# Twenty short TensorE trains, read by nothing, behind the last store of an attention-and-FFN kernel

## The chip, the core and the metric

The kernel runs on one core of one Trainium2 chip. The metric is device time in microseconds (us) of one execution, and the figure before is the median of two runs. A profile was taken of one further execution; its time and its span (from the first to the last instruction) are given below. Engines: PE is TensorE's matmul, PEld its weight load, DVE is VectorE, ACT is ScalarE, POOL is GpSimd, SP is SyncE, which issues most of the DMA transfers.

## The reference

A per-head dynamic convolution over 7 neighbouring rows (8 x 4096 rows of 192 numbers, 8 heads, weights by a softmax over the 7 taps), and then a feed-forward layer with a squared ReLU. Everything is in 32-bit floats.

```python
w = exp(weight_gen - max); w = w / (sum(w) + 1e-09)          # 8 x 4096 x 8 heads x 7 taps
out = np.einsum('bshk,bskhg->bshg', w, x_unf)                # 7 shifted rows of x
x = out.reshape(32768, 192)
h = x @ w_in                                                 # 192 x 2048
g = np.maximum(h, 0.0) ** 2
return (g @ w_out).astype(np.float32)                        # 2048 x 192
```

## The kernel before, in words

The 32768 rows are cut into 64 chunks `c` of 512 rows. DVE makes the seven products of the convolution and adds them; a DVE transpose and a trip through DRAM turn the result so that the 192 features lie on partitions. For each chunk there are two matrix products:

- `mm1(c, j)` (line 446), for 8 values of `j`: `x @ w_in`, into two PSUM banks of the pool `ps_h` (four banks, tile `ph`).
- `mm2_turned(c, fb)` (line 519), for 16 values of `fb`: `g @ w_out`, into the four banks `acc0` to `acc3` of the pool `ps_o`.

Every number is kept as a high part and a low part in the type `fp32r`, so that a product is three matmuls (high by high, low by high, high by low). `W` holds `w_in` and `V` holds `w_out` in that form; `gh`, `gl` and `xh`, `xl` are the activations. Each matmul uses only 64 of TensorE's 128 rows: the work is issued in pairs, one matmul on partitions 0 to 63 and one on 64 to 127, into two different banks. Both halves are told by `h` (or `i`) in

```python
for h in range(2):
    rows = slice(h * D1, (h + 1) * D1)
    nc.tensor.matmul(accs[c][b + h], w, two_streams(g[rows]), **fl)
```

The moving operand, 512 columns, isn't read in the order of its addresses, but in two streams that take turns, 16 numbers (64 bytes) apart:

```python
def two_streams(t):
    return t.rearrange("p (b i m) -> p b m i", i=2, m=Q // 2)
```

So the columns come from the addresses 0, 16, 1, 17, 2, 18 and so on up to 15, 31, and then on in the next 32 numbers. The last chunk's second product is not turned: `mm2` (`mm2_tile`, line 492) holds the activations fixed on all 128 rows and moves `V` in the order of its addresses, 384 columns against the high part and 192 against the low part. In chunk 0 `mm2_tile` (line 483) does it in plain `fp32`, 192 columns at a time.

The program is written in the order in which each engine takes it (a manual schedule; no scheduler changes it). At its end stand, on PE, four matmuls at line 784 and eight at line 787 (192 columns each, all 128 rows); then a DVE addition (line 790), and `store(c, t, TC)`, the last of the output's DMA transfers (line 78). After that all engines meet and the program ends. `D1` is 64, `P` 128, `N` 512, `NF` 16, `D` 192, `Q` 32; `ghs[NCH - 1, NF - 1]` is the last high part of the last chunk, `accs[NCH - 1][0]` its bank `acc0`.

Of the kernel before, what the change touches and what calls it, by code (L numbers as in the profile page):

```python
# [8 lines left out]
F32 = mybir.dt.float32  # L9
# [12 lines left out]
def kernel(  # L22
# [547 lines left out]
    def store(c, t0, t1):  # L570
        put_out(c, t0, t1, outs[c][0], 1 if c == 0 else 0)
# [218 lines left out]
    nc.vector.tensor_tensor(out=o_sb[:, t], in0=rest[:, 0:D], in1=tmp[:, t, 0:D], op=ALU.add)  # L790
    store(c, t, TC)


# [1 line left out]
_INS = ["x", "weight_gen", "moe_w_in", "moe_w_out"]  # L795
# [26 lines left out]
```

## Time and profile before

| | us |
|---|---|
| median of 2 runs | 2129.09 (2128.73 to 2129.44) |
| profiled execution, its time | 2128.85 |
| profiled execution, its span | 2126.9 |
| PE busy in the span | 2121.8 |
| DVE busy | 1864.2 |
| ACT busy | 1797.9 |
| mean granted TensorE clock | 1.000 |

Time lies outside the span too: 2128.85 less 2126.9. A matmul's end is modelled in the profile, and matmuls overlap in the pipeline, so the busy time of PE doesn't tell its rate; the distance from one start to the next does.

### The profile page before, as it was taken

Reading aid. Unit: us, or ns where it says so; the run is one execution under the profiler, and the core shown is the slowest. Engines: PE = TensorE matmul, PEld = TensorE weight load, DVE = VectorE, ACT = ScalarE, POOL = GpSimd, SP = SyncE. Lnnn points to the kernel's source line nnn. Section 1 sums busy time; section 2 is a strip of 40 time slices with the busy share of each in tenths; the row PEclk is TensorE's granted clock in tenths of the full one; section 3 lists DMA queues with packets and bytes.
Section 4 is the critical chain, followed back from the end, with each engine's and each line's share of the span. In section 5 each row is a group of like instructions: output and inputs, shape, how many; then the busy total and the mean of one; then the engine's idle time right before and its main releaser. Section 6 shows DMA issues by size and latency. Waiting matters only on the chain.

```text
span 2126.9 us, 50423 instructions
## 1 busy us (share of the span) xinstructions
PE 2121.8 (100%) x19486; PEld 1865.2 (88%) x19486; DVE 1864.2 (88%) x2869; ACT 1797.9 (85%) x3492; POOL 9.9 (0%) x18
## 2 busy tenths in 40 slices
PE   9999999999999999999999999999999999999999
PEld 9888888888888888888888888888888888888888
DVE  9988888888888888888888888888888888888884
ACT  8888888888888888888888888888888888888886
POOL 0000000000000000000000000000000000000000
PEclk9999999999999999999999999999999999999999
DMA  8433334333343343433434433344334343333422
GB/s 231 99 72 85 92 97 102 86 69 100 91 100 92 65 104 86 99 94 67 100 87 98 105 78 77 91 100 100 86 70 104 87 99 91 68 101 86 100 66 49
DMA packets 324160, 195.33 MB, mean 92 GB/s; under 512 B 224984, under 2 KB 282328, under 8 KB 320080
## 3 DMA queue, kind: packets, MB, share of 16 engines
q1 hardware_dynamic: 322624, 188.58, 35.9%
q0 software_dynamic: 1296, 3.54, 0.9%
q8 instruction: 152, 2.49, 0.5%
q14 instruction: 88, 0.72, 0.1%
HBM read 106.39 MB, written 49.55 MB: 73 GB/s over the span
## 4 chain that ended last, share of the span: by engine, by line
PE 99%; ACT 0%; POOL 0%; issue 0%; DVE 0%; POOLq 0%
PE acc L519 50%; PE ph L446 46%; PE acc L483 1%; PE acc L492 1%; PE acc L446 0%; PE acc L355 0%; PE acc L581 0%; ACT rg L467 0%; ACT gh L471 0%; PE ph L343 0%; ACT rg L461 0%; PE ph L787 0%; PE acc L343 0%; PE acc L784 0%; DVE o_sb L790 0%
## 5 line engine op out<-in xcount | busy, mean ns | idle before, releaser
L519 PE MATMUL acc<-gh,V 64*128 64x512 f32 x5952 | 976.9, 376 | 0.0
L446 PE MATMUL ph<-xh,W 64*128 64x512 f32 x6084 | 822.4, 376 | 0.3 <-ACT rg L461 0.3
L463 ACT ACTIVATE rg<-ph 128x512 f32<-128x512 f32 x992 | 539.3, 596 | 303.8 <-PE ph L446 303.8
L519 PE MATMUL acc<-gl,V 64*128 64x512 f32 x3968 | 752.7, 376 | 0.0
L475 DVE TENSOR_TENSOR gl<-rg,gh 128x512 fp32r<-128x512 f32 x1008 | 641.2, 675 | 12.8 <-ACT gh L471 12.8
L446 PEld LDWEIGHTS ph<-xh,W 64*128 64x128 f32 x6084 | 576.1, 186 | 82.3 <-issue 0.7
L519 PEld LDWEIGHTS acc<-gh,V 64*128 64x128 f32 x5952 | 563.5, 186 | 78.8
L467 ACT ACTIVATE rg<-rg 128x512 f32<-128x512 f32 x1008 | 580.3, 632 | 0.2
L471 ACT CAST gh<-rg 128x512 fp32r<-128x512 f32 x1008 | 575.8, 627 | 3.3 <-PE acc L492 3.3
L519 PEld LDWEIGHTS acc<-gl,V 64*128 64x128 f32 x3968 | 375.6, 186 | 53.1 <-DVE gl L475 0.6
L280 DVE TENSOR_TENSOR pr<-xt,wt 128x768 f32<-128x768 f32 (+1 forms) x441 | 416.6, 946 | 2.2
L446 PE MATMUL ph<-xl,W 64*128 64x512 f32 x3042 | 411.4, 376 | 0.0
L293 DVE TENSOR_TENSOR pr<-pr 128x768 f32<-128x768 f32 x366 | 348.1, 951 | 2.2
L446 PEld LDWEIGHTS ph<-xl,W 64*128 64x128 f32 x3042 | 288.3, 186 | 40.1
L324 DVE TENSOR_TENSOR xl<-xT,xh 128x512 fp32r<-128x512 f32 x186 | 117.5, 687 | 114.2 <-ACT xh L321 114.1
L529 DVE TENSOR_TENSOR raw<-acc,raw 128x512 f32<-128x512 f32 x124 | 79.9, 687 | 94.7 <-ACT raw L527 94.7
L321 ACT CAST xh<-xT 128x512 fp32r<-128x512 f32 x186 | 102.5, 623 | 0.8 <-DMA xT<-xd 0.8
L527 ACT COPY raw<-acc 128x512 f32<-128x512 f32 x124 | 66.5, 597 | 0.0
L409 DVE STREAM_TRANSPOSE xr<-pr 128x768 f32<-128x768 f32 x61 | 59.7, 978 | 2.1
L541 DVE STREAM_TRANSPOSE raw<-raw 64x512 f32<-64x512 f32 x62 | 43.6, 703 | 2.1
L538 DVE STREAM_TRANSPOSE raw<-raw 128x512 f32<-128x512 f32 x62 | 43.6, 704 | 0.0
L540 DVE TENSOR_TENSOR raw<-raw 64x512 f32<-64x512 f32 x62 | 41.8, 675 | 0.0
(94 smaller groups left out, 432.9 us busy)
## 6 DMA issues: line engine op xcount, KB each, us to landing
xT<-xd SPq DMA_DIRECT2D x124, 384.0 KB
xt<-in_x_dram SPq DMA_DIRECT2D x30, 1344.0 KB
out_dram<-o_sb SPq DMA_DIRECT2D x254, 96.0 KB
xd<-xr SPq DMA_DIRECT2D x248, 96.0 KB
o_sb<-raw SPq DMA_DIRECT2D x1488, 16.0 KB
raw<-raw SPq DMA_DIRECT2D x62, 128.0 KB
wt<-in_weight_gen_dram SPq DMA_DIRECT2D x31, 224.0 KB
raw<-in_moe_w_in_dram SPq DMA_DIRECT2D x16, 192.0 KB
```

Source lines behind the costliest of these rows:

```text
L280: tt(out=dst, in0=src, in1=wf[:, t0 * H:t1 * H, k:k + 1].broadcast_to([P, m, G]), op=ALU.mult)
L293: tt(out=prs[k0], in0=prs[k0], in1=prs.pop(k), op=ALU.add)
L321: nc.scalar.copy(parts["h"][:, k, n], src[k][:, n])
L324: tt(out=parts["l"][:, k, n], in0=src[k][:, n], in1=parts["h"][:, k, n].bitcast(F32), op=ALU.subtract)
L446: nc.tensor.matmul(two[i], w, two_streams(xx[rows, k]), start=(n == 0), stop=(n == len(seq) - 1))
L463: nc.scalar.activation(r, ph, AF.Relu)
L467: nc.scalar.activation(r, r, AF.Square)
L471: nc.scalar.copy(gh, rgs[c, fb])
L475: nc.vector.tensor_tensor(out=gl, in0=rgs.pop((c, fb)), in1=ghs[c, fb].bitcast(F32), op=ALU.subtract)
L519: nc.tensor.matmul(accs[c][b + h], w, two_streams(g[rows]), **fl)
L527: nc.scalar.copy(X[:, k], acc[b])
L529: nc.vector.tensor_tensor(out=X[:, k], in0=acc[b + 1], in1=X[:, k], op=ALU.add)
```

## The change

Behind the last store twenty trains of matmuls are added (twenty calls of `train`; the first two are the kernel's own form of pairs, with and without a fresh start of the sum in each). A train is six passes; in a pass one matmul for each of the two row halves is issued, 512 columns unless it says otherwise. They write into the three other banks of `ps_h` and, in one train, into `acc0` too. Nothing reads what they write. They differ from the first in one thing each: `start=False` with sums that run on over the six passes; two pairs of banks in turn; one and the same weights each time; weights from `W`; the upper half first; the order of the halves reversed every other pass; only the lower half; only the upper half; two streams 17, 18, 20, 24 and 40 numbers apart (16 from each before both move on); two streams 256 and 264 apart, each read once through; both streams read backwards; 480 columns; 448 columns; the output written backwards. The seven trains of `streams(d)` read their moving operand from `W` instead of `gh`.

```diff
     store(c, t, TC)
 
+    sides = list(enumerate((slice(0, D1), slice(D1, P))))
+    mv = ghs[NCH - 1, NF - 1]
+    wide_mv = W.rearrange("p a j e -> p (a j e)")
+    bk = [ps_h.tile([P, N], F32, name="ph") for _ in range(3)] + [accs[NCH - 1][0]]
+
+    def train(right, left=lambda f, rows: V[rows, f % NF, 0:P], out=lambda f, h, n: bk[1 + h][:, 0:n], passes=6, start=True, hs=(0, 1)):
+        for f in range(passes):
+            for h in hs if isinstance(hs, tuple) else hs(f):
+                rows = sides[h][1]
+                r = right(rows)
+                n = 1
+                for d in r.shape[1:]:
+                    n *= d
+                nc.tensor.matmul(out(f, h, n), left(f, rows), r, start=start or f == 0, stop=start or f == passes - 1)
+
+    def streams(d, i=2, m=16, n=512):
+        def f(rows):
+            a = n // (i * m)
+            v = wide_mv[rows, 0:a * i * d].rearrange("p (a e) -> p a e", a=a)
+            return v.rearrange("p a (i d) -> p a d i", i=i)[:, :, 0:m, :]
+        return f
+
+    plain = lambda rows: two_streams(mv[rows])
+    train(plain)
+    train(plain, start=False)
+    train(plain, out=lambda f, h, n: (bk[1 + h], bk[3 * h])[f % 2][:, 0:n])
+    train(plain, left=lambda f, rows: V[rows, 0, 0:P])
+    train(plain, left=lambda f, rows: W[rows, 0, f, 0:P])
+    train(plain, hs=(1, 0))
+    train(plain, hs=lambda f: (0, 1) if f % 2 else (1, 0))
+    train(plain, hs=(0,))
+    train(plain, hs=(1,))
+    for d in (17, 18, 20, 24, 40):
+        train(streams(d))
+    train(streams(256, i=2, m=256))
+    train(streams(264, i=2, m=256))
+    train(lambda rows: two_streams(mv[rows])[:, :, ::-1, :])
+    train(lambda rows: two_streams(mv[rows, 0:480]))
+    train(lambda rows: two_streams(mv[rows, 0:448]))
+    train(plain, out=lambda f, h, n: bk[1 + h][:, ::-1])
```

No other engine gets an instruction, and none is moved. At the end of PE's program the order before and after differs as follows; the second operand behind the arrow is the weights' tile, the first the moving one, and this is the piece from the fourth train on (27 matmuls and the train with two pairs of banks stand ahead of it).

```order
+L806 MATMUL ph<-gh,V 128x512 x12
+L806 MATMUL ph<-gh,W 128x512 x12
+L806 MATMUL ph<-gh,V 128x512 x36
+L806 MATMUL ph<-W,V 128x512 x84
+L806 MATMUL ph<-gh,V 128x512 x12
+L806 MATMUL ph<-gh,V 128x480 x12
+L806 MATMUL ph<-gh,V 128x448 x12
+L806 MATMUL ph<-gh,V 128x512 x12
+L858 UNCONDITIONAL_BRANCH
```

Nothing moved there: the rows only stand behind the last of line 787. In all 228 matmuls are added, 18 trains of 12 and two of 6.

## Rows read from the trace of the kernel before

**Rows 1.** The page, busy time by engine, and the chain that ended last.

```profile
PE 2121.8 (100%) x19486; PEld 1865.2 (88%) x19486; DVE 1864.2 (88%) x2869; ACT 1797.9 (85%) x3492; POOL 9.9 (0%) x18
...
PE 99%; ACT 0%; POOL 0%; issue 0%; DVE 0%; POOLq 0%
```

**Rows 2.** Stretch 200 to 2000: us, PE busy (matmuls), granted clock, DMA share, GB/s.

```profile
200.00:2000.00 1800.00, 1800.00 (x16684) 1.00 0.37 90
```

**Rows 3.** Timeline about 1000: start, us from first start to last end, engine, operation.

```profile
1000.42 0.38 PE L519 MATMUL acc<-gh,V 64*128 64x512 f32 x2
1000.42 0.19 PEld L519 LDWEIGHTS acc<-gl,V 64*128 64x128 f32 x2
1000.64 0.38 PE L519 MATMUL acc<-gl,V 64*128 64x512 f32 x2
1000.64 0.41 PEld L519 LDWEIGHTS acc<-gh,V 64*128 64x128 f32 x4
1000.85 0.38 PE L519 MATMUL acc<-gh,V 64*128 64x512 f32 x2
```

**Rows 4.** Timeline of the last chunk's second product, the moving operand in order of addresses.

```profile
2105.16 0.25 PE L492 MATMUL acc<-V,gl 128*128 128x192 f32 x1
...
2105.26 0.36 PE L492 MATMUL acc<-V,gh 128*128 128x384 f32 x1
...
2105.45 0.25 PE L492 MATMUL acc<-V,gl 128*128 128x192 f32 x1
...
2105.54 0.36 PE L492 MATMUL acc<-V,gh 128*128 128x384 f32 x1
```

**Rows 5.** Groups of matmuls by line and shape: busy us, mean ns of one, idle before.

```profile
L519 PE MATMUL acc<-gl,V 64*128 64x512 f32 x3968 | 752.7, 376 | 0.0
...
L492 PE MATMUL acc<-V,gh 128*128 128x384 f32 x60 | 17.2, 360 | 0.0
L492 PE MATMUL acc<-V,gl 128*128 128x192 f32 x60 | 14.6, 252 | 0.0
L483 PE MATMUL acc<-du,gl 128*128 128x192 f32 x64 | 10.7, 326 | 0.0
```

**Rows 6.** Timeline of PE where chunk 0 ends, from 128-row to 64-row matmuls.

```profile
53.12 0.98 PE L483 MATMUL acc<-du,gl 128*128 128x192 f32 x5
54.02 0.92 PE L446 MATMUL ph<-xh,W 64*128 64x512 f32 x6
```

**Rows 7.** Timeline at the end, up to the last store.

```profile
2122.49 0.27 PE L787 MATMUL ph<-V,gh 128*128 128x192 f32 x1
...
2123.07 1.23 SPq L78 DMA_DIRECT2D out_dram<-o_sb  x2
...
2123.16 0.27 PE L787 MATMUL ph<-V,gh 128*128 128x192 f32 x1
...
2123.27 0.27 PE L787 MATMUL ph<-V,gl 128*128 128x192 f32 x1
2123.58 0.36 DVE L790 TENSOR_TENSOR o_sb<-ph,raw 128x192 f32<-128x192 f32 x1
```

**Rows 8.** Last stretches: us, busy us of PE, PEld, DVE, ACT, POOL, clock, DMA share, GB/s.

```profile
2124.00:2124.50 0.50, 0.00 (x0) 0.00 (x0) 0.00 (x0) 0.00 (x0) 0.00 (x0) 1.00 0.50 161
2124.50:2125.00 0.50, 0.00 (x0) 0.00 (x0) 0.00 (x0) 0.00 (x0) 0.00 (x0) 1.00 0.35 115
2125.00:2125.50 0.50, 0.00 (x0) 0.00 (x0) 0.00 (x0) 0.00 (x0) 0.00 (x0) 0.99 0.26 82
2125.50:2126.00 0.50, 0.00 (x0) 0.00 (x0) 0.00 (x0) 0.00 (x0) 0.00 (x0) 0.50 0.00 0
2126.00:2126.90 0.90, 0.00 (x0) 0.00 (x0) 0.00 (x0) 0.00 (x0) 0.00 (x0) 0.50 0.00 0
```

## The prediction, written before the changed kernel was run

> **What bounds the kernel now.** I read the page first. PE is busy for 2121.8 of 2126.9 us and the chain that ended last is 99% PE [rows 1]: nothing that another engine does could hide matmuls that are put behind PE's last one, except what the program still does after it. So two readings decide the forecast: how long one pair of matmuls takes in this form, and how much of the end of the program the trains lie beside.
>
> For the pair I don't use PE's busy time. The mean of one matmul is 376 ns [rows 5], but its end is modelled and pairs overlap. The distance of starts is what counts: in the stretch from 200 to 2000 us, where PE does nothing but these pairs, 16684 matmuls, that is 8342 pairs, take 1800 us, or 0.2158 us a pair [rows 2]. The timeline shows the same: pairs start at 1000.42, 1000.64, 1000.85, and the two halves of a pair stand in one row as x2 [rows 3], so they run side by side. [...]
>
> For the end I read the last 4 us. The last matmul starts at 2123.27, DVE's last addition runs from 2123.58 to 2123.94 [rows 7], and then the last store goes out; DMA traffic is there until 2125.5 and gone after it [rows 8]. The last 1.4 us, up to 2126.9, hold no work of any engine: all engines meet there. Between PE's last start and the end of the span lie 3.63 us.
>
> **The change part by part.** It removes and moves nothing. It adds 228 matmuls with their weight loads on PE, and nothing on the other engines or queues. SP's last transfers and DVE's addition don't wait for them. The trains read `gh`, `V` and `W`, which were written long before, and write banks whose readers were done long before (the three other `ph` banks were read in the last chunk's first product; `acc0` was read first of the four), so I take no wait on another engine and count 0 for it; were there one, it would be for DVE's last read, up to 2123.94, and cost at most 0.6 us.
>
> The start: matmuls of 192 columns on 128 rows start 0.11 us apart at the end (2123.16, 2123.27 [rows 7]), so the first train may start at 2123.38. It goes from 128-row to 64-row matmuls. Where chunk 0 ends the same happens: the five of line 483 start 0.163 us apart, since (0.98 - 0.326) / 4 is 0.163 [rows 5, 6], the last of them thus at 53.77, and the next starts at 54.02, 0.09 us later than the step would have it; the six matmuls after that take 0.92 us, where three pairs at the steady step take 2 x 0.216 + 0.38 = 0.81 [rows 5, 6]. I count 0.09 + 0.11 = 0.20 us for the change of form, with 0 as the lower bound.
>
> The trains whose pairs differ from the kernel's only in banks, weights, the order of halves or `start`, seven of them, cost 6 pairs of 0.2158 us each, 1.295 us a train. In the steady stretch [rows 2] both weights and banks change too, between the pairs of one product and the next, and by the code `start` is true in the first pair of a sum alone; so these seven have one answer: 9.06 us.
>
> The two trains of one half only are 12 matmuls of 512 columns. A row half takes a new matmul each 0.2158 us in the steady stretch, and the weights of the next pair are loaded while the matmul on the same half runs: the load begins at 1000.42 and at 1000.64, in the moment in which the pair itself starts [rows 3]. So a lone half should go on at 0.2158 us a matmul. The last of the lower half and the first of the upper can run side by side, and the halves stay staggered after that, so 11 steps: 2.37 us.
>
> The two short trains: 480 and 448 columns by 0.4215 ns, six pairs each: 1.21 and 1.13 us, an estimate by the column from [rows 2].
>
> That leaves nine trains in which the pattern itself is new: the distances 17, 18, 20, 24, 40, 256, 264, the streams backwards, the output backwards. At the steady step they cost 9 x 1.295 = 11.65 us. [...] What could be lost is bounded by two kinds of rows. Read in the order of addresses, a matmul of 192 and one of 384 columns start 0.285 us apart together (2105.16 to 2105.45 and 2105.26 to 2105.54 [rows 4]): 576 columns, 0.495 ns each, 1.17 times the two-stream column, though on 128 rows and with half the columns. Plain `fp32` takes 0.163 us for 192 columns [rows 5, 6], 0.85 ns each, two cycles a column. For the five distances up to 40 I take the steady step, as they are the same picture (two streams, 16 numbers from each) as the row at distance 16, to which they are nearest. For 256, 264 and the two backward trains I take the factor 1.17, as they are the ones least like it: 4 x 1.295 x 0.17 = 0.9 us. The bounds I keep for the range: 0, and two cycles a column.
>
> [...] The row first: at distance 16, two neighbouring columns never lie in the same 64 bytes, and the pair still takes 0.2158 us [rows 2]. [...]
>
> The sum: 9.06 + 2.37 + 1.21 + 1.13 + 11.65 = 25.4 us, and 0.9 for the four odd patterns. The first train starts at 2123.38 with 0.20 of change of form. The last matmul ends 0.16 us later than its step (0.38 against 0.216 [rows 3]). So PE ends at 2123.38 + 0.20 + 25.4 + 0.9 + 0.16 = 2150.0. Then the engines meet. Behind the last transfer that took 1.4 us [rows 8], some of which may be the notice of the transfer; with PE as the last I take 1.2, between 0.7 and 1.4. Span 2151.2; with the 1.95 us that lie outside it (2128.85 less 2126.9) **2153.2 us**, 24.3 above the profiled execution and 1.1% above the median. The store, its landing and DVE's addition are wholly covered by the trains, which is why 25.4 + 0.9 us of added work cost 24.3 only. Without any of the 0.9 it is 2152.3.
>
> **The rivals.** (a) Patterns at two cycles a column, the rate of plain `fp32` [rows 5, 6]: a stream at an odd distance, or a backward read or write. 1.295 us more for each train; for four of them 2152.3 + 5.2 = 2157.5, for all nine 2164.0. For it: nothing in the trace shows that distance is free. Against: at 16, which is already far, it is. (b) The weight loads of the one-half trains aren't hidden. A weight load bounds the matmuls of line 787 at 0.11 us [rows 7]; 12 of these in the open are 1.3 us, which gives 2154.5. Against it: a load runs beside a matmul of the same half [rows 3]. [...] (c) The other side, slower by over 2%: the two streams and the two halves take turns for one memory, so that the nine new patterns cost four cycles a column: 3 x 1.295 = 3.9 us more a train, 2152.3 + 35 = 2187. It decides from 2171.7 on (1.02 x 2129.09), that is from 19.4 us more in nine trains, a pair of 0.575 us, 2.7 times the steady one. Nothing in the trace goes that slowly at the full clock. [...] (e) That the trains are left out or run ahead can be excluded: 228 matmuls stand behind line 787 in the built program.
>
> **How the numbers follow.** The forecast, all patterns between the steady step and the factor 1.17 (2151.3 to 2155): 0.75. (a) 0.14, about half of it up to 2159; (b) 0.05; (c) 0.03; (d) 0.02; the rest, something shorter than counted, 0.01. Range 2151.0 to 2159.0: it holds the forecast, (b), and the lower half of (a). Two per cent, 42.6 us, is about what a measurement of this kernel is asked to tell from no change: within 2% 0.94, slower 0.05 from (c), (d) and the worst of (a), faster 0.01, as nothing is removed.
>
> **What would show it.** In the changed profile: up to 2123.3 us nothing differs; line 806 holds 228 matmuls from 2123.4 to about 2150 with no idle time; starts of pairs 0.216 us apart in the first seven trains; matmuls of one half 0.216 apart; 0.202 and 0.189 in the short ones; the granted clock 1.00 until after the last. A pair of 0.43 us in a distance train is (a); 0.33 in a one-half train is (b). The prediction is wrong if a pattern train takes over 2.6 us, or if the steady form itself doesn't reach 0.216 us here.

## The result, and the profile after

| | before | after |
|---|---|---|
| median, us | 2129.09 (2 runs) | 2151.74 (2151.63 to 2151.86, 2 runs) |
| ratio | | 1.0107, 95% interval 1.0090 to 1.0124 |
| profiled execution: time, span | 2128.85, 2126.9 | 2151.86, 2149.9 |

Slower by 22.65 us, 1.1%: within 2%, but clear of the noise. The forecast was 2153.2, 1.5 us too high, in a range of 2151.0 to 2159.0.

The page after, busy time by engine: PE has 228 matmuls and 25.3 us more than in [rows 1], DVE nothing.

```profile
PE 2147.1 (100%) x19714; PEld 1888.8 (88%) x19714; DVE 1864.2 (87%) x2869; ACT 1796.8 (84%) x3492; POOL 9.9 (0%) x18
```

The timeline after, around the last store and at the very end; it answers to [rows 7].

```profile
2123.49 0.28 PE L787 MATMUL ph<-V,gl 128*128 128x192 f32 x1
...
2123.69 2.64 PE L806 MATMUL ph<-gh,V 64*128 64x512 f32 x22
2123.80 0.36 DVE L790 TENSOR_TENSOR o_sb<-ph,raw 128x192 f32<-128x192 f32 x1
...
2148.62 0.38 PE L806 MATMUL ph<-gh,V 64*128 64x512 f32 x1
```

The last matmul of the old work starts at 2123.49, 0.22 later than in the profiled execution before, less than the two executions before differ by (0.71). The first train starts 0.20 us behind it, and DVE's last addition runs beside it: no wait was added on either side. The next view is the windows of the same trace at the end (columns as in [rows 8]).

```profile
2125.00:2125.70 0.70, 0.70 (x10) 0.62 (x8) 0.00 (x0) 0.00 (x0) 0.00 (x0) 1.00 0.44 141
2125.70:2126.50 0.80, 0.80 (x10) 0.69 (x10) 0.00 (x0) 0.00 (x0) 0.00 (x0) 1.00 0.00 0
2126.50:2148.60 22.10, 22.10 (x205) 21.17 (x202) 0.00 (x0) 0.00 (x0) 0.00 (x0) 1.00 0.01 1
2149.00:2149.90 0.90, 0.00 (x0) 0.00 (x0) 0.00 (x0) 0.00 (x0) 0.00 (x0) 1.00 0.00 0
```

The last store has landed by 2125.7, as before, with 23 us of trains still to come. The granted clock stays at 1.00 to the end, where in [rows 8] it fell to 0.50 two us after PE had stopped. The last matmul starts at 2148.62 and ends at 2149.0; 0.9 us later the span ends.

The timeline at the two one-half trains holds the surprise. Before this stretch stand the seven trains of pairs, behind it the train with distance 17, the first that moves `W`; in the order of the program every `ph<-gh` here stands ahead of every `ph<-W`. A view merges like neighbours into one row; the first two rows are from narrow windows at 2133.05 and 2133.24.

```profile
2132.86 0.38 PE L806 MATMUL ph<-gh,V 64*128 64x512 f32 x1
...
2133.07 0.38 PE L806 MATMUL ph<-gh,V 64*128 64x512 f32 x1
...
2134.16 0.39 PE L806 MATMUL ph<-W,V 64*128 64x512 f32 x1
2134.26 0.38 PE L806 MATMUL ph<-gh,V 64*128 64x512 f32 x1
2134.38 0.40 PE L806 MATMUL ph<-W,V 64*128 64x512 f32 x1
2134.48 0.38 PE L806 MATMUL ph<-gh,V 64*128 64x512 f32 x1
```

Matmuls of the distance train start at 2134.16 and 2134.38, each before a matmul of the upper-half train that stands ahead of it in the program (2134.26 and 2134.48). The view doesn't name the half; I tell it by the rhythm, as two sequences of starts about 0.216 us apart run side by side here. The early ones belong to the lower half, which had nothing else left to do. So a row half doesn't wait for the other half's turn in the program. A lower matmul starts at 2132.86 and the next at 2133.07, alone: a lone half goes on at 0.216 us a matmul, its weight loads hidden (one of 0.19 us starts at 2133.08, beside the matmul of 2133.07).

### The profile page after: what moved, and what is told of

It reads as the page before. It is cut to its first block, busy times and chain, and to the rows that moved or that the text cites. A ratio compares the mean times of both kernels' runs of the same rounds, so it can differ in the third digit from the quotient of the medians.

```text
span 2149.9 us, 50881 instructions
## 1 busy us (share of the span) xinstructions
PE 2147.1 (100%) x19714; PEld 1888.8 (88%) x19714; DVE 1864.2 (87%) x2869; ACT 1796.8 (84%) x3492; POOL 9.9 (0%) x18
## 4 chain that ended last, share of the span: by engine, by line
PE 99%; ACT 0%; DMA 0%; DVE 0%; SPq 0%; issue 0%; DVEq 0%
PE acc L519 50%; PE ph L446 46%; PE ph L806 1%; PE acc L483 1%; PE acc L492 1%; PE acc L446 0%; PE acc L355 0%; DMA xt<-in_x_dram 0%; ACT rg L467 0%; ACT gh L471 0%; PE ph L343 0%; ACT rg L461 0%; PE ph L787 0%; PE acc L343 0%; DVE pr L280 0%; PE acc L784 0%
```

## The experiments

Each is the changed kernel with other trains behind the same last store, but for e7, which is the kernel before with one edit. Nothing reads what the trains write. e3, e4, e5b and e6 were run once each; what is read from them are distances between starts within one trace, at a granted clock of 1.00. A pair's step is (start of the next train less start of this one) / 6. Timeline rows read: start, us from first start to last end, how many.

**One train, and twenty alike.** e1 keeps the first train alone; e8 makes all twenty like the first.

```diff
     train(plain)
-    train(plain, start=False)
...
-    train(plain, out=lambda f, h, n: bk[1 + h][:, ::-1])
```

> Only the first train stays (12 matmuls, 6 pairs). Cover theory: PE then ends at about 2123.3 + 0.1 + 0.2 + 1.3 + 0.2 = 2125.1 us, before the last store has landed (2125.5), so the time is that of the kernel before, 2129.1, within 0.3 us. Rival, the trains count from their first matmul on: 1.3 to 1.5 us more, 2130.4 to 2130.6. If the first holds, what the trains cost in the changed kernel is what reaches beyond the landing, and the end after the last of them is about 0.9 us.

Measured: 2129.06 us in 11 runs against 2129.15 in 15 of the kernel before, ratio 1.000 (0.9991 to 1.0008). The interval alone is too wide to exclude 1.3 us; the trace settles it. Its timeline and windows at the end:

```profile
2123.66 0.27 PE L787 MATMUL ph<-V,gl 128*128 128x192 f32 x1
...
2123.86 1.56 PE L806 MATMUL ph<-gh,V 64*128 64x512 f32 x12
2123.97 0.36 DVE L790 TENSOR_TENSOR o_sb<-ph,raw 128x192 f32<-128x192 f32 x1
...
2125.50:2126.00 0.50, 0.00 (x0) 0.00 (x0) 0.00 (x0) 0.00 (x0) 0.00 (x0) 1.00 0.07 20
2126.00:2127.30 1.30, 0.00 (x0) 0.00 (x0) 0.00 (x0) 0.00 (x0) 0.00 (x0) 1.00 0.00 0
```

PE is done at 2125.42, the store's traffic lasts into the window from 2125.5, and the span ends 3.6 us after the start of the last old matmul (2123.66 to 2127.3), as before (3.63). The first train is free.

> The change with all twenty trains made like the first (240 matmuls, 120 pairs). If the sum of the changed kernel is understood: 18 trains as there, and in place of the one-half trains' 1.83 us two full ones of 2.59, of the short ones' 2.35 us 2.59, and 0.13 us less for the distances 17 and 18: 0.87 us more than the changed kernel, 2152.6. In the trace 119 steps of 0.2158 us from the first start to the last, and 0.10 more at the first: 25.8 us, and 1.3 us from the last start to the end of the span. In-order theory with the prediction's 2.37 us for the one-half trains: 0.33 more, 2152.1. If other patterns of the change had cost something hidden, less than 2152.

Measured: 2152.78 us (4 runs), 1.04 above the changed kernel where 0.87 was expected and 0.33 was the rival's. The timeline has all 240 in one row:

```profile
2123.93 26.17 PE L806 MATMUL ph<-gh,V 64*128 64x512 f32 x240
```

26.17 less the last matmul's own 0.38 is 25.79 us from first start to last: 119 steps of 0.2158 and 0.10 more at the first, as expected. So the steady step of [rows 2] holds for the trains to the last digit, and what the changed kernel has less comes from its other patterns.

**Without the one-half trains.** e2:

```diff
-    train(plain, hs=(0,))
-    train(plain, hs=(1,))
```

> The change without its two trains of one row half (12 matmuls fewer). Lane theory (each row half takes its matmuls on its own, up to four waiting matmuls ahead, and a lane that stood empty pays 0.10 us for a weight load in the open): 1.83 us less than the changed kernel, 2149.9. In-order theory (matmuls start in the order of the program, as the prediction had it, 11 steps): 2.37 us less, 2149.4. Weight loads in the open in each of the 12: 3.9 us less, 2147.8. In the trace the two halves of a pair start within 4 ns of each other up to the end, where in the changed kernel they are 0.11 us apart after the one-half trains; the distances 17 and 18 then show 0.234 and 0.220 a pair.

Measured: 2150.10 us (4 runs), 1.64 less than the changed kernel: nearer to 1.83 than to 2.37, but with a spread of 0.5 us. The trace decides. Three trains of it (distances 17, 18, 20) and the last:

```profile
2132.51 1.56 PE L806 MATMUL ph<-W,V 64*128 64x512 f32 x12
...
2133.90 1.49 PE L806 MATMUL ph<-W,V 64*128 64x512 f32 x12
...
2135.23 1.46 PE L806 MATMUL ph<-W,V 64*128 64x512 f32 x12
...
2145.35 1.46 PE L806 MATMUL ph<-gh,V 64*128 64x512 f32 x12
```

From the first start (2123.34) to the last (2145.35 + 1.46 - 0.38 = 2146.43) are 23.09 us; in the changed kernel, 2123.69 to 2148.62, 24.93. The difference is 1.84, the lane theory's number. The pairs stand undisturbed here, so each pattern can be read: distance 17 takes 0.232 a pair, 18 takes 0.221, and 20, 24, 40, 256, 264, backwards and the backward output all 0.216; 480 columns 0.2025, 448 columns 0.189.

**Blocks of one half.** e3 lets blocks of `b` matmuls of one half take turns with `b` of the other.

```diff
+    for b in (2, 3, 4, 6, 8, 24):
+        train(plain, hs=lambda f: (0,) * b + (1,) * b, passes=24 // b)
+        train(plain)
+    train(plain, passes=24)
```

> Trains in which blocks of 2, 3, 4, 6, 8 and 24 matmuls of the lower row half take turns with as many of the upper half, 24 for each half in all, a train of pairs between them, and 24 pairs at the end; 420 matmuls, 210 for each half. By steps of 0.2158 us, last start plus one step: lanes with a window of four waiting matmuls 230 steps, 49.6 us (blocks of 2, 3 and 4 lose nothing, 6 loses 2 steps, 8 loses 4, 24 loses 20) and some 0.1 us for each time a lane stood empty; matmuls in the order of the program 287 steps, 61.9 us (2 loses 1, 3 loses 9, 4 loses 13, 6 loses 17, 8 loses 19); a window of 32 matmuls 210 steps, 45.3 us, no loss even at 24.

Measured, from the timeline, and PE's windows inside the blocks of 2, 8 and 24 (stretch, us, busy and the matmuls that run in it or reach into it, granted clock, DMA share, GB/s):

```profile
2123.58 50.68 PE L806 MATMUL ph<-gh,V 64*128 64x512 f32 x420
...
2124.90:2130.00 5.10, 5.10 (x52) 1.00 0.07 23
...
2151.00:2156.90 5.90, 5.90 (x51) 1.00 0.01 3
2158.40:2167.50 9.10, 9.10 (x53) 1.00 0.00 0
```

From first start to last are 50.3 us, 50.5 with one step more: near the window of four (49.6 and 0.1 for each lane that stood empty), far from the order of the program (61.9) and from a window of 32 (45.3). By the starts in the trace, the 48 matmuls in blocks of 2, of 3 and of 4 take 5.18 us each time, as pairs do (24 steps of 0.2158), and those in blocks of 24 take 8.86, where one half alone would take 10.4. I replayed the list of 420 by three rules: a half takes its next matmul when its last one is 0.2158 us old; only the first W matmuls that haven't started are looked at; a half that stood empty, or that comes from 128-row matmuls as at the first pair, takes 0.104 us more for its second. With W = 4 every one of the 420 starts comes out within 0.12 us; with W = 3 they are off by up to 2.5 us, with W = 5 by 1.1.

**What makes a stream fast.** e4 varies where runs of the moving operand begin, and the number of streams; e5b how often a line of 16 bytes is used before the next. e6 (below) does the 128-row form.

```diff
+    def shifted(o):
+        return lambda rows: two_streams(wide_mv[rows, o:o + 512])
+
...
+    for o in (1, 2, 3, 4, 8):
+        train(shifted(o))
+    for d in (19, 21, 22, 23):
+        train(streams(d))
+    for m in (8, 4, 2):
+        train(streams(m, m=m))
+    train(streams(8, i=4, m=8))
+    train(streams(16, i=4, m=16))
+    train(lambda rows: mv[rows])
...
```

> Twenty-one trains of pairs that differ in the moving operand's addresses alone. Line theory (a run of 16 numbers that doesn't begin at a multiple of four numbers, 16 bytes, touches a fifth line, and that costs): distance 16 begun 1, 2 or 3 numbers later 0.220 to 0.234 us a pair, begun 4 or 8 later 0.216; distances 19, 21, 22, 23 0.220 to 0.234; two streams 8 or 4 apart in runs of 8 or 4 0.216; in runs of 2 (all in one line) like the order of addresses. Distance theory (only the distance of the streams counts, 17 and 18 are too odd): the shifted ones all 0.216, 19 to 23 0.220 to 0.234. In the order of addresses I expect 0.25 (the factor 1.17 of the last chunk's second product) if that order is what costs there, 0.216 if it is the 128 rows; every second number 0.25 or more, every fourth (each in a line of its own) up to 0.43.

Its timeline, one row a train: begun 3, 4 and 8 numbers later; distance 19; four streams of 8 and of 16; order of addresses; the same begun one later; every second number; every fourth; and the next.

```profile
2128.63 1.51 PE L806 MATMUL ph<-W,V 64*128 64x512 f32 x12
...
2129.98 1.46 PE L806 MATMUL ph<-W,V 64*128 64x512 f32 x12
...
2131.27 1.46 PE L806 MATMUL ph<-W,V 64*128 64x512 f32 x12
...
2132.57 1.56 PE L806 MATMUL ph<-W,V 64*128 64x512 f32 x12
...
2142.07 1.77 PE L806 MATMUL ph<-W,V 64*128 64x512 f32 x12
...
2143.68 1.78 PE L806 MATMUL ph<-W,V 64*128 64x512 f32 x12
...
2145.30 1.54 PE L806 MATMUL ph<-gh,V 64*128 64x512 f32 x12
...
2146.67 1.58 PE L806 MATMUL ph<-W,V 64*128 64x512 f32 x12
...
2148.09 2.87 PE L806 MATMUL ph<-W,V 64*128 64x512 f32 x12
...
2150.78 2.95 PE L806 MATMUL ph<-W,V 64*128 64x512 f32 x12
...
2153.55 1.58 PE L806 MATMUL ph<-gh,V 64*128 64x512 f32 x12
```

Begun 3 later is 0.225 a pair (1.35 / 6), 1 and 2 later 0.227 and 0.224 from the same view; 4 and 8 later 0.215 and 0.216; the distances 19, 21, 22 and 23 0.224 to 0.234. So it isn't the distance: what costs is a run that doesn't begin on a multiple of four numbers. The distance theory falls with the shifted rows. Order of addresses is 0.229, neither the 0.25 nor the 0.216 that I had expected, and 0.236 begun one later; two streams 2 apart in runs of two 0.232, four streams 0.268. Every second number is 0.449, every fourth 0.461, more than the 0.43 I had thought the most.

Every second and every fourth number cost nearly the same though one uses twice as many numbers of a line. That suggested the use theory of e5b. It supposes that the engine takes two columns at a time (one taking), and that what counts is how many takings in a row a line serves. The trains of the diff read the numbers 0 0 1 1 2 2; 0 to 3 twice; 0 to 7 twice; 0 4 1 5 8 12; 0 512 2 514; 0 1 256 257 2 3; 0 to 3 and 256 to 259; runs of two from four streams; and eight streams.

```diff
+    train(each_twice)
+    train(twice(4))
+    train(twice(8))
+    train(lambda rows: wide_mv[rows, 0:1024].rearrange("p (b i e) -> p b e i", i=2, e=4)[:, :, 0:2, :])
+    train(lambda rows: long(1024, "p (i m s) -> p m i s", i=2, s=2)(rows)[:, :, :, 0])
+    train(long(512, "p (i m s) -> p m i s", i=2, s=2))
+    train(long(512, "p (i m s) -> p m i s", i=2, s=4))
+    train(long(512, "p (i m s) -> p m i s", i=4, s=2))
+    train(streams(16, i=8))
...
```

> Twelve trains of pairs, 512 columns, in which a line of four numbers (16 bytes) is used a different number of times before the next. Use theory (the engine takes two columns at a time; a line that serves four takings in a row costs nothing, 0.216 us a pair; one that serves two and then changes costs 6%, 0.229; one that serves one only costs double, 0.45): each number twice (0, 0, 1, 1) 0.216; four numbers twice (0 to 3, 0 to 3) 0.216; eight numbers twice 0.229; two neighbouring lines by 0, 4, 1, 5 and then on to the next two 0.229; every second number in two streams 512 apart 0.229; two streams in runs of two, 0, 1, 256, 257, 2, 3: 0.27 to 0.45; in runs of four 0.229; four streams in runs of two 0.27 or more; eight streams 0.27 or more; order of addresses 0.229. Stream theory (two lines in turn are what is fast): the repeats 0.229; 0, 4, 1, 5 and the runs of two and of four 0.216. Use-of-numbers theory (a line of which half is left out costs): every second number in two streams 0.45.

Its timeline, in the order of the diff, from the first of these trains on:

```profile
2125.13 1.46 PE L806 MATMUL ph<-W,V 64*128 64x512 f32 x12
...
2126.43 1.46 PE L806 MATMUL ph<-W,V 64*128 64x512 f32 x12
...
2127.72 1.60 PE L806 MATMUL ph<-W,V 64*128 64x512 f32 x12
...
2129.16 1.55 PE L806 MATMUL ph<-W,V 64*128 64x512 f32 x12
...
2130.54 1.54 PE L806 MATMUL ph<-W,V 64*128 64x512 f32 x12
...
2131.91 2.19 PE L806 MATMUL ph<-W,V 64*128 64x512 f32 x12
...
2133.93 1.67 PE L806 MATMUL ph<-W,V 64*128 64x512 f32 x12
...
2135.44 2.88 PE L806 MATMUL ph<-W,V 64*128 64x512 f32 x12
...
2138.12 2.83 PE L806 MATMUL ph<-W,V 64*128 64x512 f32 x12
```

Each number twice 0.216; four numbers twice 0.216; eight twice 0.240; 0 4 1 5 0.231; every second in two streams 0.228; runs of two 0.337; runs of four 0.251; four streams in runs of two 0.447 (eight streams 0.44). The order of addresses, once more, 0.236. One stream alone can thus be as fast as two, if each line serves four takings; the stream theory falls with the first two rows, the use-of-numbers theory with the fifth. The use theory has the order right: four takings in a row 0.216, two 0.228 to 0.251, one 0.268 to 0.461. It doesn't have the sizes: eight twice and runs of four are 0.01 to 0.02 above its 0.229, and why, among the patterns of one taking, four streams (0.268) and two in runs of two (0.337) lie so far below the others stays open. That columns are taken two at a time is a supposition that fits; no run shows it by itself.

**The 128-row form, and outputs.** e6 repeats the last chunk's product in trains, once in the order of addresses and once in two streams, and then writes outputs in two streams of runs of 2, 4 and 16.

```diff
+                r = V[:, f % NF, 0:n] if n < N else mv
+                nc.tensor.matmul(bk[1 + f % 2][:, 0:n], g[:, 0:P], two_streams(r) if two else r, start=True, stop=True)
```

> Trains on all 128 rows as the last chunk's second product has them (12 passes of 384 and 192 columns, or one of them, or 512), in the order of addresses and in two streams, and pairs whose output is written in two streams of runs of 2, 4 and 16. Order theory (the order of addresses costs 0.285 us for 576 columns): in two streams 0.245 to 0.25; 384 alone 0.175 to 0.20 in order, 0.163 in streams; 512 alone 0.229 and 0.216; 192 alone 0.11 both, by the weight load. Rows theory (128 rows or the weight loads cost it): 0.285 both ways. [...]

Timeline: 384 and 192 columns in turn in two streams; then 384 alone in order and in streams.

```profile
2129.48 0.35 PE L820 MATMUL ph<-V,gh 128*128 128x384 f32 x1
...
2129.75 0.36 PE L820 MATMUL ph<-V,gh 128*128 128x384 f32 x1
...
2131.67 2.30 PE L820 MATMUL ph<-V,gh 128*128 128x384 f32 x12
...
2133.82 2.11 PE L820 MATMUL ph<-V,gh 128*128 128x384 f32 x12
```

In turn, two streams give 0.273 us (2129.48 to 2129.75), the order of addresses 0.285 as in [rows 4]. Alone, 384 columns take 0.179 in order and 0.162 in streams ((2.11 - 0.33) / 11); 192 alone 0.111 either way, and 512 alone 0.231 and 0.216. So neither theory: 0.273 is 0.162 and 0.111, and the order of addresses adds 0.011. The 0.111, which doesn't depend on the order, I take for a weight load that 192 columns (0.081 us at 0.4215 ns) are too short to cover; no run varies the load alone. The outputs in runs of 2, 4 and 16 all took 0.216.

**Reading the last chunk in two streams.** e7, without trains:

```diff
-            (acc[:, 0:2 * D], ghs[c, fb][:, ts_], V[:, fb]),
-            (acc[:, 0:D], gls[c, fb][:, ts_], V[:, fb, 0:D]),
+            (acc[:, 0:2 * D], ghs[c, fb][:, ts_], two_streams(V[:, fb])),
+            (acc[:, 0:D], gls[c, fb][:, ts_], two_streams(V[:, fb, 0:D])),
...
-                nc.vector.tensor_tensor(out=to[:, h], in0=acc[:, h], in1=tmp[:, t, l], op=ALU.add)
+                nc.vector.tensor_tensor(out=two_streams(to[:, h]), in0=taken(acc[:, h]), in1=taken(tmp[:, t, l]), op=ALU.add)
...
```

> The kernel before, without trains, with the last chunk's second product (lines 492, 784, 787) reading its moving operand in two streams, and DVE putting the columns back in order as it adds. Order theory: 60 pairs of matmuls at 0.245 to 0.25 in place of 0.285 us, 2.1 to 2.4 us less, 2126.7 to 2127.0. Rows theory: no change, 2129.1. Rival: by 0.25 us a pair PE catches up with ACT's and DVE's making of the next operands (a CAST each 1.14 us and a subtraction, for four pairs), so that part of it turns into waits: 0.5 to 1.5 us less.

Measured: 2128.70 us (11 runs) against 2128.80 (15), ratio 0.9999 (0.9990 to 1.0008): no gain that can be told, where the order theory had 2.1 to 2.4 us. The start of this product before, and then its start and the end of the timeline in e7:

```profile
2104.88 0.45 PE L492 MATMUL acc<-V,gh 128*128 128x384 f32 x1
...
2105.74 0.43 PE L495 MATMUL acc<-V,gh 128*128 128x384 f32 x1
...
2123.50 0.28 PE L790 MATMUL ph<-V,gl 128*128 128x192 f32 x1
2123.85 0.48 DVE L793 TENSOR_TENSOR o_sb<-ph,raw 128x192 f32<-128x192 f32 x1
```

From the first start of this product to PE's last, 2105.74 to 2123.50, are 17.76 us; before, 2104.88 to 2123.27, 18.39. The 0.63 us are there, 60 pairs of 0.0105, but DVE's last addition in the new order takes 0.48 in place of 0.36 us, and what is left, some 0.5 us, is less than two executions differ by: the product itself starts anywhere from 2104.74 to 2105.93 in the ten traces.

## Why the prediction was right, and where its terms were not

The direction and the bulk followed from two readings. PE's last instruction sets the end, and trains behind it are covered until the store lands and count one for one after that: e1 shows the cover (2129.06 against 2129.15 us), e8 the step. The step of 0.2158 us from [rows 2] was exact (e8).

| term | predicted, us | measured | from |
|---|---|---|---|
| last old matmul to first train | 0.20 | 0.20 | 2123.49 to 2123.69 |
| first step's extra | 0.11 | 0.10 | e8 |
| seven trains of the known form | 9.06 | 9.06 | e2 |
| one-half trains | 2.37 | 1.84 | e2 |
| 480 and 448 columns | 2.34 | 2.35 | e2 |
| distances 17 to 40, above the step | 0 | 0.13 | e2 |
| 256, 264 and the two backward ones, above it | 0.9 | 0 | e2 |
| end of PE to end of span | 1.2 | 0.9 | after |

The differences add up to 1.6 us too much; the profiled execution was 0.2 us later at the start of the trains; that leaves, within rounding, the 1.34 us between 2153.2 and its 2151.86. The number held although several terms were wrong, and nearly all in the same direction, because each was off by less than 1 us; that is luck of size, not a sign that those steps were right.

- The largest miss is the step "for 256, 264 and the two backward trains I take the factor 1.17". [rows 4] was a wrong witness: 576 columns at 0.4215 ns are 0.243 us, so it loses 0.042; some three quarters of that stay when the order of addresses goes (e6, argued there to be a weight load that 192 columns don't cover), and only 0.011 is the order. In pairs that order costs 6% (0.229), and none of the four is read in that way: all begin on lines of four numbers and use each line four times.
- "For the five distances up to 40 I take the steady step": right for 20, 24 and 40; 17 and 18 don't begin on a line, and cost 8% and 2%. I judged by likeness to distance 16 and should have looked at the remainder by four.
- "11 steps" for the one-half trains assumed that matmuls start in the order of the program. They don't: a matmul that stood third in line started first (2134.16, ahead of 2134.26 and 2134.48), the upper half began when the third lower matmul did, and the two halves ran side by side for the rest (after, e2, e3). Rival (b), weight loads in the open, was wrong; the lone half went on at 0.216, in the blocks of 24 of e3 for over 3 us on end. That a weight load sets the 0.11 us of [rows 7], from which (b) was priced, was my estimate: no run varies the load alone.
- Of the rivals (a) and (c) nothing was seen: the slowest pattern of the change was 0.234 a pair. What the 0.02 of (d) stands for, a lower granted clock during the trains, no run shows: it stayed at 1.00. Patterns at twice the steady step and more do exist (0.449 and 0.461 a pair, e4); the change has none.

One bound was misread: "two cycles a column", from "plain `fp32` takes 0.163 us for 192 columns", is the rate of one instruction and not of one `fp32` matmul. [rows 5] shows 64 instructions of line 483 with `gl`, the same view has 64 more with `gh`, and the program has 64 matmuls there in all (16 values of `fb`, four tiles):

```profile
L483 PE MATMUL acc<-du,gh 128*128 128x192 f32 x64 | 10.7, 328 | 0.0
```

So a plain `fp32` matmul goes as two instructions, 0.325 us for 192 columns, 1.69 ns a column, four times the 0.4215 ns of [rows 2] (0.2158 us for 512 columns). Rival (a) rested on that price, the forecast didn't. A cycle in these prices stands for the 0.4215 ns; no run shows the length of a clock cycle. The range's bound of 0 for the new patterns supposes that no column goes faster, and no run shows such a floor: the fastest measured take 0.42 ns a column.

What the new patterns cost goes by lines of 16 bytes: begun 4 or 8 numbers later 0.215 and 0.216, 1 to 3 later 0.224 to 0.227 (e4). If a taking is two columns, two takings of a line in a row cost 6% to 16% (0.228 to 0.251), four cost nothing (0.216), and one costs up to double (0.45). At distance 16 each line serves four takings, though two neighbouring columns never share a line, and a pair takes 0.2158 [rows 2]. Outputs that are written backwards (e2) or in runs of 2, 4 and 16 (e6) cost nothing: 0.216.

## What to carry to other kernels

Work behind the last store costs only what reaches beyond the store's landing, here a train of 1.3 us for nothing (e1), and then its full length. (The span ends 1.4 us behind the landing before and 0.9 us behind the last matmul after, so by estimate the cover reaches some 0.5 us past the landing; no run ended there.) Price a matmul's pattern by the 16-byte lines of its moving operand: begin runs on multiples of four 32-bit numbers and let a line serve four takings of two columns (e5b's supposition; two streams at a multiple of four numbers, 4 to 264 tried), and it ran here at 0.4215 ns a column; the order of addresses cost 6% to 9% (0.229 to 0.236 a pair), one taking a line up to double the time (0.268 to 0.461). Before a row of another form is used as a price, ask which of its parts, the load of the weights or the reading, set it (576 columns took 0.285 us, and the order of reading was 0.011 of it, e6).

## What the runs showed of the hardware that I had not expected

- The two 64-row halves of TensorE take their matmuls each on its own, out of the order of the program, among the first four that haven't started: 420 starts within 0.12 us by that rule (e3). Blocks of up to four matmuls of one half cost nothing against pairs (5.18 us for 48, either way).
- A half that stood empty loses 0.104 us at its second matmul: the upper half's second start in its one-half train comes 0.320 us behind its first (after, 2133.30 to 2133.62), in place of 0.216. So does a pair's behind 128-row matmuls (0.10 more at the first step of e8).
- Reading every second 32-bit number (0.449 us a pair) is as slow as every fourth (0.461), while every second one in two streams takes 0.228.
